# A second read of k in the last phase: its place in the DMA queue, and the rank of the gram's products on VectorE

## The chip, the cores and the metric

The kernel runs on one core of one Trainium2 chip. Its time is device microseconds of one execution, and the time that counts is the median of several. A core has TensorE (matrix products and transposes, into PSUM), VectorE and ScalarE (elementwise work, and copies out of PSUM), GpSimd (POOL; here little more than constants), and SyncE (SP), whose queue issues nearly all DMAs. An engine takes its instructions in the order in which the program has them, and so does a queue: an instruction that waits holds up what is behind it.

## The reference

The function is a residual block with two branches on a normalised input, and its gradients. S = 2048 rows, D = 512 channels, F = 1376 hidden channels, all in bf16:

```python
xn = layernorm(x)                                     # x = A_q
ks[s, d] = sum_j k[s - j, d] * shift_k[d, j]          # j = 0..3, a short causal filter
kv = ks * v
y = causal_convolution(kv, ssm_k) + kv * ssm_D        # over s, by FFT
A = xn * y
h = (xn @ w_gate) * (xn @ w_up)
B = h @ w_down
out = x + A + B
```

Ten tensors are returned: `out`, and for a given `grad_out` the gradients of x, k, v, shift_k, ssm_k, ssm_D and of the three weights. The part that matters here is the gradient of `shift_k`. With `dks` = d(loss)/d(ks), it is

`d_shift_k[d, j] = sum over s of dks[s, d] * k[s - j, d]`.

## The kernel before, in words

Sequence rows are spread over the 128 partitions, 16 consecutive rows (R) in each. The work has three stages: loading, normalising and the forward part of the convolution's transform; the hidden products of the second branch, block by block, with the spectral products between them; and a last phase, from about 316 us on, which computes the gradients of the weights.

In the last phase a generator `dw()` goes through 11 blocks (FBLK) of 128 hidden channels. For each it issues products for the gradient of `w_down` (`down_grad`, tile `pd`, L996), turns the hidden tensors of the next block by transposes (`hid_t`, tile `pt`, L840; from the loaded tile `hb`, two buffers, loaded at L787 two blocks ahead), and issues products for the gradients of `w_gate` and `w_up` (tile `pu`, L1032), which ScalarE copies to `og` (one buffer) and SP stores (L1043). `dw()` yields several times in a block, and at these points pieces of four other generators are put between, by a list `sides` of starting step and spacing:

- `inv_y` (from step 0, every third): the last step of the inverse transform, for four rows at a time. It takes the tiles `g1` (`load_g1`, L781, two buffers), first of y and then of the gradient `dd`, issues products `pq` (L913), and for the gradient VectorE forms `dks` = dd * v (L945) and `kb` = dd * ks (L946), which SP stores (L947). v and ks come by `load_vk` (L918, L920; two buffers). Eight g tiles are used so, two at a time; after them `load_dk` asks for the first two of four more.
- `dsk_gram` (from step 27, every second): the gradient of `shift_k`, for 128 channels at a time, two halves of 64 each. TensorE multiplies `dks` with four shifted views of k (tile `khC`, of 19 rows a partition: 16 of its own and 3 of the partition before) into a PSUM tile `pk` (L1055). The gradient is the diagonal of that product, so VectorE multiplies it by the identity, one product for each half (`kd`, L1060), and sums (L1062).
- `inv_dk` (from step 35): the gradient of the long filter `ssm_k`, from the four last g tiles (`po`, L971, into `o5t`). Its tile `o5t` has the memory of `khC` after it.
- `ew` (from step 10): `final(b)` (L1105 to L1122), the layer norm's backward pass and `out`, for two rows a piece, with a tile `bb` that it loads one piece ahead (L1094), and `bwd(b)` (L1084 to L1088), the gradient of k from `dks`. Both are VectorE's work, and SP stores what they make.

PSUM has a pool of three large buffers (`P2`), which `pu`, `pk`, `pt`, `pq` and `po` take in turn, and a pool of two smaller ones (`P1`, for `pd` and others). A tile's next user waits until the engine that reads it out has finished.

The order on each engine and queue is worked out at build time by a planner: it goes by the place in which an instruction is traced, as its priority, and by its own estimate of when things are ready. `tc.high_priority(offset=SOON)`, with SOON = 300, lets the instructions of a block count as if they had been traced 300 places earlier. `tc.issue_after(i)` adds the order that what the block issues on i's engine comes behind i; it does not say how soon.

`khC` is loaded by `load_kh` (L1126): a small memset on POOL and three requests on SP, 2048 KB for the rows themselves and 336 and 45 KB for the three rows from the partition before. `inv_y` calls it in its last pass, behind that pass's four requests of `load_vk`.

Of the kernel before, what the change touches and what calls it, by code (L numbers as in the profile page):

```python
# [11 lines left out]
ALU = mybir.AluOpType  # L12
ACTF = mybir.ActivationFunctionType
AX = mybir.AxisListType
# [6 lines left out]
R = 16  # L21
# [5 lines left out]
SOON = 300  # L27
# [163 lines left out]
def kernel(  # L191
# [24 lines left out]
    nc = tc.nc  # L216
# [20 lines left out]
    def dve(o, i):  # L237
        nc.vector.tensor_copy(o, i)  # L238
# [6 lines left out]
    GD = dram.tile([3, P, 2, R, D], BF, name="GD")  # L245
# [12 lines left out]
    ident = const.tile([P, P], BF, name="ident")  # L258
# [519 lines left out]

    def load_g1(sg, r0):
        t = CP["b"].tile([P, 2, 4, D], BF, name="g1")  # L780
        nc.sync.dma_start(t[:], GD[sg, :, :, r0:r0 + 4, :])  # L781
        return t

    def load_hb(fb):
        f0, fw = FBLK[fb]
        t = CP["b"].tile([P, NCH - 1, 3, 256], BF, name="hb")
        nc.sync.dma_start(t[:fw], HDD[:fw, fb])  # L787
        hbs[fb] = t
# [118 lines left out]
    dsk = c2.tile([P, NC4, 4], F32, name="dsk")  # L907
# [8 lines left out]
    def load_vk(r0):  # L916
        vb = c2b.tile([P, 2, D], BF, name="vb")
        nc.sync.dma_start(vb[:], v_n[:, r0:r0 + 2, :])  # L918
        kb = c2b.tile([P, 2, D], BF, name="kb")
        DKS["kb", r0] = nc.sync.dma_start(kb[:], KS[:, r0:r0 + 2, :])  # L920
        return vb, kb

    DKS = {}

    def inv_y():
        gq = pend
        todo = [(sg, r0) for r0 in range(0, R, 4) for sg in (0, 1)][2:]
        for r4 in range(0, R, 4):
            gy = gq.pop(0)
            vk = [load_vk(r4), load_vk(r4 + 2)]  # L930
            if r4 == R - 4:
                load_kh()
            for i in range(0, 4, 2):
                st1p(gy, i, yC[:, r4 + i:r4 + i + 2, :])
            if todo:
                gq.append(load_g1(*todo.pop(0)))
            yield
            gd = gq.pop(0)
            for i in range(0, 4, 2):
                r0 = r4 + i  # L940
                vb, kb = vk.pop(0)
                dd = c2b.tile([P, 2, D], BF, name="dd")
                st1p(gd, i, dd[:])
                with tc.high_priority(offset=SOON):
                    nc.vector.tensor_tensor(dks[:, r0:r0 + 2, :], dd[:], vb[:], op=ALU.mult)  # L945
                    nc.vector.tensor_tensor(kb[:], dd[:], kb[:], op=ALU.mult)  # L946
                DKS[r0] = nc.sync.dma_start(o3_n[:, r0:r0 + 2, :], kb[:])  # L947
                if r0 == 2:
                    nc.gpsimd.memset(dks[96:128, R:R + 3, :], 0.0)
                    nc.sync.dma_start(dks[0:112, R:R + 3, :], dks[1:113, 0:3, :])  # L950
                    nc.sync.dma_start(dks[112:127, R:R + 3, :], dks[113:128, 0:3, :])
            if todo:
                gq.append(load_g1(*todo.pop(0)))
            yield

    def load_gk(rq):
# [92 lines left out]
    def dsk_gram():  # L1049
        for c in range(NC4):  # L1050
            pk = P2("pk", [P, 2, D])
            for r in range(R):
                for h in range(2):
                    c0 = c * 128 + 64 * h
                    nc.tensor.matmul(pk[64 * h:64 * h + 64, h, 0:256], lhsT=dks[:, r, c0:c0 + 64],  # L1055
                                     rhs=KH[0][:, r:r + 4, c0:c0 + 64], start=(r == 0), stop=(r == R - 1))
            kd = c2.tile([P, 4, 64], F32, name="kd")
            for h in range(2):
                hs = slice(64 * h, 64 * h + 64)
                nc.vector.tensor_tensor(kd[hs], pk[hs, h, 0:256].rearrange("q (j c) -> q j c", j=4),  # L1060
                                        ident[hs, hs].unsqueeze(1).to_broadcast((64, 4, 64)), op=ALU.mult)
            nc.vector.tensor_reduce(dsk[:, c, :], kd[:], axis=AX.X, op=ALU.add)  # L1062
            yield
        dskb = c2.tile([P, 4, NC4], BF, name="dskb")
        nc.vector.tensor_copy(dskb[:], dsk[:].rearrange("q c i -> q i c"))
        for _ in range(2):
            yield
        pt = P1("pts", [P, 4, P], BF)
        for j in range(4):
            nc.tensor.transpose(pt[:NC4, j, :], dskb[:, 3 - j, :], ident[:])  # L1070
        dskt = c2.tile([NC4, P, 4], BF, name="dskt")
        dve(dskt[:], pt[:NC4].rearrange("c j q -> c q j"))
        nc.sync.dma_start(out_4.rearrange("(c p) j -> c p j", p=128), dskt[:])
        yield
# [51 lines left out]
    def load_kh():  # L1126
        khC = c2.tile([P, R + 3, D], BF, name="khC", tag="o5k")
        nc.gpsimd.memset(khC[0:1, 0:3, :], 0.0)
        with tc.issue_after(DKS["kb", R - 2].ins):
            nc.sync.dma_start(khC[:, 3:3 + R, :], k_n)  # L1130
            nc.sync.dma_start(khC[1:113, 0:3, :], k_n[0:112, R - 3:R, :])
            nc.sync.dma_start(khC[113:128, 0:3, :], k_n[112:127, R - 3:R, :])
        KH.append(khC)
# [63 lines left out]
```

## Time and profile before

| | |
|---|---|
| median of 3 runs | 487.18 us (486.45 to 489.52) |
| profiled execution | 485.22 us, span 483.4 us |
| TensorE busy (PE) | 471.3 us, 97% |
| VectorE busy (DVE) | 340.4 us, 70% |
| ScalarE busy (ACT) | 317.6 us, 66% |
| HBM traffic | 68.45 MB read, 63.41 MB written |
| granted TensorE clock | full throughout |

PE stands for TensorE's products, PEld for its weight loads, SPq for SP's queue. A row of the timeline has the start in us, the duration in us, the engine, the line, the operation, and the tiles as out<-in; in brackets, how long the engine stood idle ahead of it and what ended that. A row of waits has who waited, for what, the sum in us, how often, and the longest. The chain that ended last is the work followed back from the end, at each step to what released it. A row by stretches has the stretch, its length, the busy time of each engine with the number of instructions, the granted clock, the busy share of the DMA engines and the GB/s that they moved. For a DMA the time to landing counts from its issue.

### The profile page before, as it was taken

The page shows a single profiled execution, that of the slowest core. Times are in us where ns is not written, and L with a number is a line of the kernel's source. Part 1 is how long each engine was busy: PE and PEld are TensorE (multiplying, and loading weights), DVE is VectorE, ACT ScalarE, POOL GpSimd, SP SyncE. Part 2 cuts the span into 40 slices and gives each one's busy share as a digit, 9 for nine tenths or more (in the row PEclk, how much of TensorE's full clock was granted, in tenths as well). Part 3 has the DMA queues.
Part 4 walks back from the last instruction along what each step waited for, and adds up shares of the span by engine and source line. Part 5 has one row for each costly group of instructions (what it writes and reads, how often), then busy time and mean ns, then how long its engine had stood idle before and what let it go on. Part 6 is the DMA issues. An engine that isn't in the chain of part 4 may idle for free.

```text
span 483.4 us, 10516 instructions
## 1 busy us (share of the span) xinstructions
PE 471.3 (97%) x4335; PEld 314.5 (65%) x4335; DVE 340.4 (70%) x622; ACT 317.6 (66%) x354; POOL 15.3 (3%) x31
## 2 busy tenths in 40 slices
PE   7998998999999999999999999999999999999997
PEld 7866754647638547447447743566777787787885
DVE  7889969989275567686767866013257999999880
ACT  4976896759748778779779976275676535344241
POOL 8010000000000000000000000020000000000000
PEclk9999999999999999999999999999999999999999
DMA  9999998998997968967977378999999999599737
GB/s 269 378 381 354 294 263 298 353 311 315 327 288 260 263 201 269 280 203 248 287 238 262 119 270 317 381 329 313 318 383 380 320 374 414 199 250 241 229 147 247
DMA packets 105469, 139.87 MB, mean 289 GB/s; under 512 B 33323, under 2 KB 78800, under 8 KB 103758
## 3 DMA queue, kind: packets, MB, share of 16 engines
q1 hardware_dynamic: 103838, 137.84, 86.6%
q10 hardware_dynamic: 1584, 1.36, 1.0%
q8 instruction: 34, 0.56, 0.4%
q14 instruction: 13, 0.11, 0.1%
HBM read 68.45 MB, written 63.41 MB: 273 GB/s over the span
## 4 chain that ended last, share of the span: by engine, by line
PE 79%; DVE 9%; DMA 8%; ACT 1%; SPq 1%; issue 1%; DVEq 0%; ACTq 0%
PE pu L1032 15%; PE px L553 14%; PE pgu L510 13%; PE pd L996 7%; PE py L546 7%; PE pdh L516 6%; PE pt L840 4%; PE pq L913 3%; PE ps L582 3%; PE pg L611 3%; PE pf L368 2%; DMA HDD<-hd 2%; DVE fst L238 2%; PE pk L1055 2%; DMA out_dram<-og 1%; DMA kh<-in_A_k_dram 1%
## 5 line engine op out<-in xcount | busy, mean ns | idle before, releaser
L553 PE MATMUL px<-WT,hd 128*128 128x512 bf16 (+1 forms) x352 | 81.0, 380 | 0.0
L1032 PEld LDWEIGHTS <-xnC 128*128 128x128 bf16 x704 | 67.1, 98 | 8.8 <-issue 0.9
L553 PEld LDWEIGHTS <-hd 128*128 128x128 bf16 (+1 forms) x352 | 32.8, 98 | 44.2 <-issue 7.3
L1032 PE MATMUL pu<-natd,xnC 128*128 128x256 bf16 x512 | 58.5, 273 | 0.2 <-ACT nath L235 0.2
L235 ACT CAST GO<-pg 128x1024 bf16<-128x1024 f32 x48 | 46.2, 1015 | 13.4 <-issue 6.7
L598 DVE TENSOR_TENSOR T<-SP 128x2048 bf16<-128x2048 bf16 x24 | 29.3, 1222 | 34.8 <-ACT SP L235 34.8
L510 PE MATMUL pgu<-xt,Wu 128*128 128x256 bf16 (+1 forms) x352 | 53.2, 273 | 0.6 <-DVE fst L238 0.4
L235 ACT CAST gu<-pgu 128x1024 bf16<-128x1024 f32 (+1 forms) x48 | 45.4, 945 | 12.5 <-PE pgu L510 12.0
L235 ACT CAST SP<-ps 128x1024 bf16<-128x1024 f32 x48 | 46.5, 1027 | 10.3 <-PE ps L582 8.4
L510 PE MATMUL pgu<-xt,Wg 128*128 128x256 bf16 (+1 forms) x352 | 52.8, 273 | 0.0
L516 PE MATMUL pdh<-gt,WdT 128*128 128x256 bf16 (+1 forms) x352 | 47.1, 273 | 0.1
L510 PEld LDWEIGHTS <-Wu 128*128 128x128 bf16 (+1 forms) x352 | 33.0, 100 | 14.7 <-issue 10.2
L546 PE MATMUL py<-Wd,hd 128*128 128x512 bf16 (+1 forms) x176 | 41.4, 380 | 0.0
L235 ACT CAST og<-pu 128x1024 bf16<-128x1024 f32 (+1 forms) x11 | 10.9, 993 | 44.9 <-PE pu L1032 28.9
L235 ACT CAST fst<-pf 128x1024 bf16<-128x1024 f32 x40 | 39.0, 1032 | 0.8 <-ACT dh L235 0.5
L235 ACT COPY natd<-pt 128x2048 bf16<-128x2048 bf16 x16 | 30.0, 1874 | 13.1 <-PE pt L840 13.1
L516 PEld LDWEIGHTS <-WdT 128*128 128x128 bf16 (+1 forms) x352 | 34.9, 100 | 5.2 <-issue 0.2
L510 PEld LDWEIGHTS <-Wg 128*128 128x128 bf16 (+1 forms) x352 | 34.8, 100 | 3.9 <-DMA Wg<-in_B_w_gate_dram 0.3
L530 DVE TENSOR_TENSOR hd<-gu 128x512 bf16<-128x512 bf16 (+1 forms) x48 | 19.1, 397 | 19.5 <-ACT gu L235 19.5
L531 DVE TENSOR_TENSOR hd<-gu,dh 128x1024 bf16<-128x1024 bf16 (+1 forms) x48 | 30.8, 641 | 0.9
L996 PE MATMUL pd<-goC,nath 128*128 128x512 bf16 x128 | 30.1, 379 | 0.0
L546 PEld LDWEIGHTS <-hd 128*128 128x128 bf16 (+1 forms) x176 | 16.4, 98 | 20.5 <-issue 3.1
(171 smaller groups left out, 698.1 us busy)
## 6 DMA issues: line engine op xcount, KB each, us to landing
HDD<-hd SPq DMA_DIRECT2D x35, 384.0 KB, 4.2
FD<-fst SPq DMA_DIRECT2D x24, 512.0 KB, 4.8
X<-FD SPq DMA_DIRECT2D x24, 512.0 KB, 4.8
GD<-GO SPq DMA_DIRECT2D x24, 512.0 KB, 3.6
g<-GD SPq DMA_DIRECT2D x12, 1024.0 KB, 8.3
hb<-HDD SPq DMA_DIRECT2D x8, 1344.0 KB, 7.6
bb<-BX SPq DMA_DIRECT2D x8, 512.0 KB, 8.3
BX<-bx SPq DMA_DIRECT2D x7, 512.0 KB, 3.8
```

Source lines behind the costliest of these rows:

```text
L235: nc.scalar.copy(o, i)
L510: nc.tensor.matmul(pgu[:w, i, t, :], lhsT=W[:, c, f0:f0 + w], rhs=xt[:, :, c, :], start=(c == 0), stop=(c == NC4 - 1))
L516: nc.tensor.matmul(pdh[:w, i, :], lhsT=WdT[:, c, f0:f0 + w], rhs=gt[:, :, c, :], start=(c == 0), stop=(c == NC4 - 1))
L530: nc.vector.tensor_tensor(hd[:fw, fb0:fb0 + n, 0, :], gu[:fw, :n, 0, :], gu[:fw, :n, 1, :], op=ALU.mult)
L531: nc.vector.tensor_tensor(hd[:fw, fb0:fb0 + n, 1:3, :], gu[:fw, :n], dh[:fw, :n].unsqueeze(2).to_broadcast((fw, n, 2, 256)), op=ALU.mult)
L546: nc.tensor.matmul(py[:], lhsT=hd[:fw, fb, 0, ss], rhs=Wd[:fw, fb, :], start=(fb == 0), stop=(fb == NFB - 1))
L553: nc.tensor.matmul(px[:], lhsT=hd[:fw, fb, t, ss], rhs=W[:fw, fb, :], start=(t == 1 and fb == 0), stop=(t == 2 and fb == NFB - 1))
L582: nc.tensor.matmul(ps[32 * q:32 * q + 32, a, :], lhsT=TB.EF[64 * a:64 * a + 64, 4 * g + q, ri].rearrange("p k j -> p (k j)"), rhs=X[64 * a ...
L598: tt(W[:].rearrange("p c a d -> p c (a d)"), A[:, i:i + 1].rearrange("p c a d -> p c (a d)").to_broadcast((P, 2, 2 * D)), B[:].rearrange(" ...
L840: nc.tensor.transpose(pt[:, r, :fw], hs[:, (r % 2) * 128:(r % 2) * 128 + 128], ident[:fw, :fw])
L996: nc.tensor.matmul(pd[:fw, :], lhsT=nat_h(fb, r), rhs=goC[:, r, :], start=(r == 0), stop=(r == R - 1))
L1032: nc.tensor.matmul(pu[:, c, :, :fw], lhsT=xnC[:, r, cs(c)], rhs=nat_d(fb, r), start=(r == 0), stop=(r == R - 1))
```

## The change

There are two edits. `load_kh` is called one pass of `inv_y` earlier, at the end of the pass for rows 8 to 11, and its requests on SP are ordered behind the load of g that was traced last, in place of the last `kb` load of the last pass. At that point this load is the eighth and last g tile of `inv_y`, for the gradient of rows 12 to 15; the four of the long filter come later. The second edit puts the two products with the identity and the sum behind them, in each of the four pieces of `dsk_gram`, under `high_priority(offset=SOON)`. The arithmetic is the same.

```diff
     def load_g1(sg, r0):
         t = CP["b"].tile([P, 2, 4, D], BF, name="g1")
-        nc.sync.dma_start(t[:], GD[sg, :, :, r0:r0 + 4, :])
+        LG["g"] = nc.sync.dma_start(t[:], GD[sg, :, :, r0:r0 + 4, :])
         return t
+
+    LG = {}
...
         for r4 in range(0, R, 4):
             gy = gq.pop(0)
             vk = [load_vk(r4), load_vk(r4 + 2)]
-            if r4 == R - 4:
-                load_kh()
...
             if todo:
                 gq.append(load_g1(*todo.pop(0)))
+            if r4 == R - 8:
+                load_kh()
             yield
...
             kd = c2.tile([P, 4, 64], F32, name="kd")
-            for h in range(2):
-                hs = slice(64 * h, 64 * h + 64)
-                nc.vector.tensor_tensor(kd[hs], pk[hs, h, 0:256].rearrange("q (j c) -> q j c", j=4),
-                                        ident[hs, hs].unsqueeze(1).to_broadcast((64, 4, 64)), op=ALU.mult)
-            nc.vector.tensor_reduce(dsk[:, c, :], kd[:], axis=AX.X, op=ALU.add)
+            with tc.high_priority(offset=SOON):
+                for h in range(2):
+                    hs = slice(64 * h, 64 * h + 64)
+                    nc.vector.tensor_tensor(kd[hs], pk[hs, h, 0:256].rearrange("q (j c) -> q j c", j=4),
+                                            ident[hs, hs].unsqueeze(1).to_broadcast((64, 4, 64)), op=ALU.mult)
+                nc.vector.tensor_reduce(dsk[:, c, :], kd[:], axis=AX.X, op=ALU.add)
             yield
...
         nc.gpsimd.memset(khC[0:1, 0:3, :], 0.0)
-        with tc.issue_after(DKS["kb", R - 2].ins):
+        with tc.issue_after(LG["g"].ins):
             nc.sync.dma_start(khC[:, 3:3 + R, :], k_n)
```

## The prediction

> **What bounds the kernel now.** I read the page first: which engine is full, then the chain that ended last, then the last phase alone.
>
> ```profile
> span 483.4 us, 10516 instructions
> PE 471.3 (97%) x4335; PEld 314.5 (65%) x4335; DVE 340.4 (70%) x622; ACT 317.6 (66%) x354; POOL 15.3 (3%) x31
> ...
> PE 79%; DVE 9%; DMA 8%; ACT 1%; SPq 1%; issue 1%; DVEq 0%; ACTq 0%
> ```
>
> TensorE has work for 97% of the span and carries 79% of the chain. So a wait is worth something only where TensorE itself stands still. The list of waits for 386 to 484 us, where all products of the gram lie, has two waits of that kind:
>
> ```profile
> PE pt L840 <- DVE kd L1060: 0.7, 1, 0.7
> ...
> PE pu L1032 <- ACT nath L235: 0.2, 1, 0.2
> ```
>
> Shifted k is not in that list: no product waited for it. It is in time by little, though. The queue's timeline has the large request (L1130) at 379.44 us, and khC's rows show 10.4 us from issue to landing, so about 390.3 us; the first `pk` product starts at 391.35. The margin is 1.0 us in this execution.
>
> The 0.7 us is at 404.69, where a transpose needs the PSUM buffer of the second gram. VectorE's timeline shows why it is late (columns: start, duration, engine, line, instruction):
>
> ```profile
> 400.80 1.42 DVE L1119 SCALAR_TENSOR_TENSOR dxn<-xnC,m,dxn 128x512 f32<-128x512 bf16 x2
> 402.13 1.00 DVE L1120 TENSOR_SCALAR e<-dxn,rstd,m 128x512 bf16<-128x512 f32 x2
> 403.17 0.42 DVE L1060 TENSOR_TENSOR kd<-pk,ident 64x256 f32<-64x256 f32 x1
> 403.50 0.67 DVE L1121 TENSOR_TENSOR e<-e,goC 128x1024 bf16<-128x1024 bf16 x1
> 404.21 0.43 DVE L1060 TENSOR_TENSOR kd<-pk,ident 64x256 f32<-64x256 f32 x1
> ```
>
> The gram's products ended at 398.68; the two `kd` products ran behind work of `final(3)` and freed the buffer at 404.64. Everything that edit two can win in this execution is that 0.67 us.
>
> Third, the DMA rings, since edit one moves 2.49 MB (2048 + 336 + 45 KB). Of the table by stretches, in which the last two numbers are the DMA engines' busy share and the GB/s:
>
> ```profile
> 366.00:376.00 10.00, 10.00 (x98) 7.38 (x96) 8.13 (x19) 8.06 (x7) 0.00 (x0) 1.00 1.03 381
> ...
> 376.00:382.00 6.00, 6.00 (x48) 4.41 (x46) 5.86 (x10) 2.17 (x3) 0.00 (x0) 1.00 0.77 225
> ```
>
> Before 376 us the rings are full; behind it they have slack, and that is where shifted k is asked for today. The change takes it out of the slack and puts it into the full stretch.
>
> **The change part by part.** *Edit one: three requests of SP move up.* The g load after which they are now issued goes out at 364.86 (1.30 us), so they stand at about 366.2 to 367.6, ahead of these, and of the `vb` and `kb` at 377.5 to 379.0:
>
> ```profile
> 366.21 1.06 SPq L1094 DMA_DIRECT2D bb<-BX  x1
> 369.17 0.33 SPq L1107 DMA_DIRECT2D out_dram<-o  x1
> 369.60 0.60 SPq L787 DMA_DIRECT2D hb<-HDD  x1
> 375.64 0.33 SPq L1122 DMA_DIRECT2D out_dram<-e  x1
> ```
>
> The three issues cost SP 0.43 + 0.44 + 0.66 = 1.5 us; only `bb` moves by it, since `o` and `hb` waited longer than that for other things. The small POOL memset ran at 323.9, far ahead, and needs nothing new. What counts is the transfer: 2.49 MB at the 381 GB/s of that stretch is 6.5 us (5.9 at 424, the row of 374 to 376; 7.9 at 315, that of 370 to 372). Between 383 and 388, while shifted k's bytes move today, requests of 256 KB take 8.0 and 9.7 us to land; such requests at 409 to 412 take 4.9 and 3.6. So what is asked for behind it waits. [...]
>
> Step by step, with 6.5 us added:
> - the g load itself is ahead and lands as before, 364.86 + 8.3 = 373.2; its product starts at 376.33. No cost.
> - `bb` of `final(2)`: 366.21 + 8.3 = 374.5 becomes about 381. VectorE uses it at 377.33, so VectorE stops for some 3.5 us unless the planner has put other work there.
> - `hb` of block 5: 369.60 + 8.7 = 378.3 becomes 384.8. TensorE turns it at 385.90. In time by 1.1 us, where today it has 7.6. At 5.9 us the margin is 1.7; at 7.9 us TensorE waits 0.3.
> - the `vb` and `kb` of rows 12 to 15 land behind `hb`: stores and loads of 0.25 + 0.13 + 4 x 0.25 MB, some 3.7 us, so about 388.5 for the last. It landed at 378.97 + 5.0 = 384.0 and was used at 384.47. VectorE is then **4 us later** than today; `dks` is complete by 389, and the gram at 391.35 still finds it.
> - shifted k lands near 380, 11 us ahead of its use. In this execution that wins nothing; in one with slower DMAs, up to what exceeds the 1.0 us.
>
> SP runs in order and its stores wait for VectorE, so `hb` of block 6 moves from 391.46 to about 395.3. It is needed at 402.97, and the rings are emptier by then (shifted k is gone from 382 to 390), so 7.6 us to landing is just enough. No cost.
>
> *Edit two: precedence for eight products and four sums.* No work is added: 8 x 0.42 + 4 x 0.41 us of VectorE move. The trace can't show where the planner will place them; bounds: unmoved in order and 4 us late, minus the 0.5 us in which VectorE stood at 395.3, the second gram frees its buffer at 408.1 (+3.4 us of TensorE's waiting over today); right behind the gram with no lateness at 399.5 (-0.67). I take a place ahead of L1119, L1120 and L1121, that is 2.33 + 0.67 = 3.0 us earlier in the order, and 3.5 us of lateness: 404.64 - 3.0 + 3.5 = 405.1. TensorE could go on at 404.02, so it waits 1.1 us: **+0.4** against today. The first, third and fourth grams free buffers that nothing waits for; three to four microseconds later they still don't.
>
> *The end.* VectorE's lateness is eaten by its idle times behind 386 us: 0.50, 0.31, 0.43, 1.18 and 0.88, together 3.3 us, all ended by stores. The last two lie behind SP's transposes, which wait for TensorE, and are safe; the others may move along. So 0.6 to 1.9 us are left at the last `dk`. Its store stands right ahead of og's:
>
> ```profile
> 469.52 0.33 SPq L1088 DMA_DIRECT2D out_dram<-dk  x1
> 469.95 0.38 SPq L1004 DMA_DIRECT2D out_dram<-od  x1
> 470.43 0.91 SPq L978 DMA_DIRECT2D out_dram<-o5t  x2
> 471.42 2.17 SPq L1043 DMA_DIRECT2D out_dram<-og  x2
> ```
>
> ScalarE's last `og` copy at 477.04 waited for that store (one buffer), and the last og store, 478.3, ends only some half a microsecond ahead of the `od` store of 480.78 that ends the run. Later by 0.6 to 1.9, it ends the run 0.1 to 1.4 later.
>
> **Sum**: TensorE +0.4, the og path +0.1 to +1.4; they run side by side, so the larger counts: I take +0.4. The profiled execution took 485.22 us (span 483.4), 1.96 below the median of the runs, 487.18. So 485.6 by its count, and **487.6** beside the median.
>
> **Rivals.**
> 1. *VectorE is late and nothing takes it up* (slower). Place: the `kd` of the second gram and the og store. Price: up to 4 - 0.5 = 3.5 us at either, so 490.7. It decides when the added transfer exceeds about 6 us and the planner leaves `kd` where it is. For it: VectorE is busy 16.2 of 17 us from 386 to 403. Against it: the two idle times of 2.06 us behind the transposes. Within it, `hb` of block 5 is late too from 7.6 us of transfer on; by the 309 GB/s of the row of 388 to 390, 8.1 us, TensorE waits 0.5 us at 385.90.
> 2. *The stall goes and nothing is late*: loads pass shifted k, or the planner fills VectorE's wait with `bwd(0)`. Then -0.67 and, without lateness, perhaps the 0.2 behind it: 486.3. For it: `bwd(0)` has some 3 us of ready work right there.
> 3. *Runs without the profiler paid for shifted k's thin margin.* Their median is 2 us above the profiled execution. If a microsecond of it is TensorE waiting at 391.35, the change wins it on top of 2: 485.5. Against it: nothing in this trace shows it.
> 4. *Nothing moves*: the planner issues k no earlier, `kd` stays: 487.2.
>
> **Chances.** Forecast (within 0.8 us of 487.6) 0.45; rival one 0.22; two 0.18; three 0.08; four 0.07. The range 485.8 to 490.0 leaves out the far end of rival one and most of three. One per cent, 4.9 us, is about what a measurement of this kernel can tell from no change: only rival one with its prices added (4 us at VectorE plus the wait for `hb`) comes there; slower by more 0.04, faster by more 0.01, within 0.95.
>
> **What would show it.** Right: shifted k asked for near 366 and landed by 381; VectorE waiting for `bb` near 377 and for `vb` or `kb` near 385; no TensorE wait at the first `pk`; a wait for `kd` near 404 of about a microsecond; the last `dk` store a microsecond later. Wrong: VectorE on time at 386, or the `kd` wait gone (rival two), or a TensorE wait on `hb` near 386 (rival one).

## The result, and the profile after

The changed kernel takes 489.38 us (median of 22 runs, 487.12 to 493.43); the kernel before, run beside it, 487.26 us (22 runs, 485.11 to 493.17). The ratio is 1.0043, with an interval of 1.0024 to 1.0063: about 2.1 us slower, clear of noise, and well inside one per cent. The profiled execution took 489.37 us, so it stands for the median; that of before (485.22) lies 2.0 us under its own. Between the two profiles there are 4.15 us, twice what the medians differ by: the profile before is of a fast execution, that after of a middling one, and this has to be kept in mind wherever the two are laid side by side.

The page of the changed kernel, its busy line and the chain that ended last by engine:

```profile
span 487.5 us, 10518 instructions
PE 473.8 (97%) x4335; PEld 315.8 (65%) x4335; DVE 340.5 (70%) x622; ACT 318.0 (65%) x354; POOL 15.4 (3%) x31
...
PE 72%; DMA 15%; DVE 9%; ACT 1%; SPq 1%; issue 1%; DVEq 0%; ACTq 0%
```

No engine got more work, since the counts are the same. TensorE is busy 2.5 us longer with the same products, and DMAs carry 15% of the chain in place of 8%. Where TensorE waits, the waits between 366 and 488 us tell (lines of L1030 and up have moved by 3, those around L840 and L971 by 2):

```profile
PE po L973 <- DMA g<-GD: 2.0, 1, 2.0
...
PE pt L842 <- DMA hb<-HDD: 0.5, 1, 0.5
...
PEld L842 <- DVE kd L1063: 0.4, 1, 0.4
```

The wait for `kd` is gone as a wait of the products. Two waits for DMAs are there in its place: 0.5 us for `hb` of block 5, and 2.0 us for the last tile of g.

**Where shifted k went.** SP's queue in the changed kernel, around the place of the edit:

```profile
365.76 0.64 SPq L781 DMA_DIRECT2D g<-GD  x1
366.45 1.74 SPq L1133 DMA_DIRECT2D khC<-in_A_k_dram  x1
...
369.63 0.38 SPq L1097 DMA_DIRECT2D bb<-BX  x1
...
377.43 0.34 SPq L1125 DMA_DIRECT2D out_dram<-e  x1
377.86 0.38 SPq L789 DMA_DIRECT2D hb<-HDD  x1
```

The three requests stand where the prediction put them, 366.45 to 369.6. The large one landed 13.7 us after its issue, at 380.1, the second at 381.4. Of the kernel before only the second's landing is known, 390.3, 10.4 us after its issue at 379.92. What the prediction did not have is the last two lines: the planner now puts the store of `e` ahead of `hb`. That store waits for VectorE, so `hb` is asked for at 377.86 in place of 369.60, and with 9.1 us to landing it comes at 387.0. By stretches (columns: stretch, length, busy time and count of each engine, granted clock, DMA share, GB/s):

```profile
366.00:376.00 10.00, 10.00 (x96) 7.18 (x94) 6.38 (x16) 8.20 (x7) 0.00 (x0) 1.00 1.04 399
376.00:382.00 6.00, 6.00 (x50) 4.60 (x48) 5.43 (x9) 2.22 (x3) 0.00 (x0) 1.00 0.99 313
```

The slack of 376 to 382 (0.77 busy, 225 GB/s before) is used up. VectorE forms the last `dks` at 391.46, in place of 383.87. The work around it is less late: 3.7 us at the end of `final(3)` (403.50 before, 407.16 after), and still 2.4 us at the last `dk`.

Not all of that is the change's doing. VectorE's first row that stands in another place than before is at 376 us. Ahead of it, at the same product of `final(2)`, it was already 1.8 us late, the first line from the kernel before, the second from the changed kernel:

```profile
367.73 0.69 DVE L1105 TENSOR_TENSOR o<-xnC,yC 128x1024 bf16<-128x1024 bf16 x1 [3.32 <-DMA out_dram<-o]
```

```profile
369.52 0.69 DVE L1108 TENSOR_TENSOR o<-xnC,yC 128x1024 bf16<-128x1024 bf16 x1 [4.21 <-DMA out_dram<-o]
```

It waits for an earlier store of `o`, which SP issued at 361.66 in place of 360.17, before it came to shifted k. So 1.5 of the 1.8 us can't come from the early request; whether the rest does isn't known. Seven profiles here are of kernels whose VectorE and SP still have the order of the kernel before at this point, that one included: they have this product between 367.73 and 370.45, and the profile before has the earliest. From there to the end of `final(3)` the changed kernel loses another 1.9 us: 1.0 because a second wait for a store of `o` is longer (1.54 us at 383.18, 0.50 at 395.77 before), and some 0.8 because `kd` work now stands ahead of it.

**Where the end comes from.** SP's queue from 433 to 459 us, in the kernel before:

```profile
433.77 0.29 SPq L1073 DMA_DIRECT2D out_dram<-dskt  x1
...
434.55 12.88 SPq L801 DMA_TRANSPOSE natT<-HDD  x2
447.52 0.54 SPq L1004 DMA_DIRECT2D out_dram<-od  x1
...
455.00 1.00 SPq L1043 DMA_DIRECT2D out_dram<-og  x2
456.09 0.56 SPq L781 DMA_DIRECT2D g<-GD  x1
```

and after:

```profile
436.87 0.29 SPq L1076 DMA_DIRECT2D out_dram<-dskt  x1
...
438.38 11.67 SPq L803 DMA_TRANSPOSE natT<-HDD  x2
450.15 0.54 SPq L1006 DMA_DIRECT2D out_dram<-od  x1
...
456.97 0.33 SPq L1091 DMA_DIRECT2D out_dram<-dk  x1
457.40 1.00 SPq L1045 DMA_DIRECT2D out_dram<-og  x2
458.49 0.55 SPq L781 DMA_DIRECT2D g<-GD  x1
```

Read it from the top. The stores of `dskt`, `e` and `o` wait for VectorE and are late. The two transposing loads behind them go in 3.8 us later and come out 2.6 us later: only 1.2 us of the lateness is taken up there. Behind them SP issues a store of `dk` (448.16 before, 450.78 after), and VectorE needs the buffer that this store frees. The first line is from before, the second from the changed kernel:

```profile
450.48 0.69 DVE L1084 TENSOR_TENSOR dk<-dks,skb 128x1024 bf16<-128x1024 bf16 x1 [1.18 <-DMA out_dram<-dk]
```

```profile
454.45 0.69 DVE L1087 TENSOR_TENSOR dk<-dks,skb 128x1024 bf16<-128x1024 bf16 x1 [1.91 <-DMA out_dram<-dk]
```

The next `dk` that VectorE finishes is stored at 456.97, and og's stores and the last load of g stand behind that, 2.4 us later than before. Before, that tile landed at 461.81, and its product started at 461.96 without a wait, with 0.15 us to spare:

```profile
461.96 1.06 PE L971 MATMUL po<-IW,g 128*128 128x128 bf16 x16
```

In the changed kernel TensorE has done what lies ahead, and stands:

```profile
461.85 0.59 PE L998 MATMUL pd<-goC,nat 128*128 128x512 bf16 x2
464.44 0.23 PE L973 MATMUL po<-IW,g 128*128 128x128 bf16 x1 [2.00 <-DMA g<-GD]
```

The wait isn't all of it. The stretches behind it, in the same columns as above:

```profile
464.00:465.00 1.00, 0.56 (x7) 0.57 (x8) 0.97 (x2) 0.05 (x1) 0.00 (x0) 0.81 0.83 310
465.00:466.00 1.00, 1.00 (x13) 1.00 (x11) 0.97 (x2) 0.00 (x0) 0.00 (x0) 0.50 0.00 0
...
467.00:468.00 1.00, 1.00 (x7) 0.67 (x5) 0.97 (x2) 0.25 (x1) 0.00 (x0) 0.50 0.00 0
468.00:469.00 1.00, 1.00 (x11) 0.89 (x10) 0.97 (x2) 0.00 (x0) 0.00 (x0) 0.99 0.56 211
```

From about 464.6 to 468.0, some 3.4 us, TensorE is granted half its clock. Measured against the same products in the profile before, it loses another 1.6 us there. So TensorE's lateness against the profile before runs like this: +0.4 us already before the place of the change (the two executions differed there), +0.7 at `hb`, -0.8 where the `kd` wait was, +2.2 at g, +1.6 in the half clock: +4.1, which is the span's 487.5 - 483.4.

### The profile page after: what moved, and what is told of

Its sections match the earlier page's. It is cut to its first block, busy times and chain, and to the rows that moved or that the text cites. A ratio compares the mean times of both kernels' runs of the same rounds, so it can differ in the third digit from the quotient of the medians.

```text
span 487.5 us, 10518 instructions
## 1 busy us (share of the span) xinstructions
PE 473.8 (97%) x4335; PEld 315.8 (65%) x4335; DVE 340.5 (70%) x622; ACT 318.0 (65%) x354; POOL 15.4 (3%) x31
## 4 chain that ended last, share of the span: by engine, by line
PE 72%; DMA 15%; DVE 9%; ACT 1%; SPq 1%; issue 1%; DVEq 0%; ACTq 0%
PE pu L1034 13%; PE px L553 13%; PE pgu L510 13%; PE py L546 6%; PE pdh L516 6%; DMA hb<-HDD 6%; PE pd L998 5%; PE pt L842 3%; PE ps L582 3%; PE pg L611 3%; PE pf L368 2%; DMA HDD<-hd 2%; DVE fst L238 2%; DMA out_dram<-o 2%; PE pk L1057 2%; PE pq L915 1%
```

## The experiments

**Theory A.** Both edits make VectorE late, and that lateness is handed on by SP's queue, which runs in order (`hb` went out 8.3 us later once it stood behind the store of `e`): stores, transposing loads, stores, the last load of g. TensorE pays at g, and pays again in clock. **Rivals:** the bytes of k alone cost, at `hb` of block 5, and g is only a symptom; the cost is in og's stores at the end; each edit has a price of its own and the two add. Each kernel was run beside the kernel before on the same chip; the rows come from four such groups of runs, so rows with another "before there" are compared by their ratios. The ratio isn't the quotient of the two medians beside it (for edit two alone that would be 1.0061). The last column counts the runs in which the mean granted clock fell below 0.999. It is a weak sign of a TensorE wait: the mean goes over the whole span, and half clock behind TensorE's last product, while the last stores land, lowers it too (to 0.998 and 0.997 in two profiles).

| kernel | median us | before there | ratio, 95% | clock below 0.999 |
|---|---|---|---|---|
| both edits (the changed kernel) | 489.38 | 487.26 | 1.0043 [1.0024, 1.0063] | 11 of 22 |
| edit one alone | 488.51 | 486.33 | 1.0029 [0.9998, 1.0059] | 8 of 12 |
| edit two alone | 489.31 | 486.33 | 1.0043 [1.0017, 1.0069] | 8 of 12 |
| both, last two g on ScalarE's queue | 489.64 | 486.33 | 1.0057 [1.0030, 1.0084] | 8 of 12 |
| before, last two g on ScalarE's queue | 490.67 | 486.33 | 1.0068 [1.0039, 1.0096] | 11 of 12 |
| before, six more products on VectorE | 492.37 | 487.24 | 1.0102 [1.0065, 1.0138] | 6 of 6 |
| both, VectorE relieved of 11 us | 486.69 | 487.24 | 0.9994 [0.9961, 1.0027] | 6 of 12 |
| before, VectorE relieved of 11 us | 486.88 | 487.24 | 0.9995 [0.9964, 1.0026] | 5 of 12 |
| both, 24 stores on POOL's queue | 516.22 | 487.24 | 1.0590 [1.0551, 1.0630] | 6 of 6 |
| both, last `po` later | 489.15 | 487.43 | 1.0030 [1.0002, 1.0057] | 11 of 12 |
| edit two, last `po` later | 487.74 | 487.43 | 0.9990 [0.9960, 1.0019] | 8 of 12 |
| before, last `po` later | 486.23 | 487.43 | 0.9973 [0.9941, 1.0005] | 3 of 12 |
| both, one of 16 rows of k loaded | 488.01 | 487.43 | 1.0008 [0.9977, 1.0039] | 5 of 12 |

The kernel before itself fell below 0.999 in 10 of 35, 6 of 23 and 15 of 35 of its runs on the three chips of the experiments, and those runs were 1.0 to 1.9 us longer in the median than its others.

### Edit one alone

The products with the identity are left as they were.

```diff
-            with tc.high_priority(offset=SOON):
-                for h in range(2):
...
+            for h in range(2):
```

> Edit one alone: shifted k asked for early, the gram's products on VectorE without precedence. Theory A (the early transfer makes VectorE late by some 3 us, SP's stores wait for VectorE, and the last load of g behind them reaches TensorE late): slower than the kernel before by 1.5 to 4 us, a TensorE wait for g of 1 to 3 us near 462 us, and besides a wait for kd near 405 of 1 us or more, since nothing moves kd forward. Rival B (what costs is the hidden tile hb of block 5, which now stands behind shifted k in the ring): slower by no more than its own wait near 387, 0.5 to 1.1 us. Rival C (the precedence reorders VectorE, and that makes the stores late): no slower than before.

The median is 2.2 us above that of before (1.4 us by the ratio), with an interval that reaches just under no change. Its profile has both DMA waits, as the list between 366 and 490 us shows:

```profile
PE po L973 <- DMA g<-GD: 2.1, 1, 2.1
...
PE pt L842 <- DMA hb<-HDD: 1.5, 1, 1.5
```

There is no wait for `kd` in it, although `kd` keeps its old rank: with `hb` 1.5 us late, TensorE comes to that transpose later itself.

### Edit two alone

```diff
-            for h in range(2):
...
+            with tc.high_priority(offset=SOON):
+                for h in range(2):
...
```

> Edit two alone: precedence for the gram's products, shifted k where it was. Theory A and rival B: faster than the kernel before by 0 to 0.7 us, the wait for kd near 404.7 gone, no TensorE wait for g beyond 0.3 us. Rival C: slower by 1 us or more, with a TensorE wait for g near 462.

Theory A expected a gain here, and so did rival B; the time is the one that rival C named, slower by 1 us or more (2.1 us by the ratio) with a wait for g. The stall for `kd` is gone; TensorE gains 0.8 us where it was. SP's queue and then TensorE's timeline of this kernel:

```profile
457.63 0.56 SPq L781 DMA_DIRECT2D g<-GD  x1
```

```profile
463.57 1.07 PE L971 MATMUL po<-IW,g 128*128 128x128 bf16 x16 [2.21 <-DMA g<-GD]
```

g is asked for 1.5 us later than before, and TensorE comes to it 0.6 us earlier. The 1.5 us don't come from the edit. VectorE was as late at 369.20 already, on a store of `o`:

```profile
369.20 0.69 DVE L1106 TENSOR_TENSOR o<-xnC,yC 128x1024 bf16<-128x1024 bf16 x1 [4.32 <-DMA out_dram<-o]
```

In this kernel SP's requests have the order of the kernel before to the end, and VectorE's instructions have it up to 401 us. From that product to the request for g there are 88.43 us here and 88.36 before. `kd` ahead of `final(3)` delays VectorE by some 0.6 us at the end of `e`, but nothing of that is left at g. So rival C's mechanism, stores made late by the new order, isn't in this profile, and neither is theory A's. What edit two changes at g is that TensorE is there earlier and finds less of a margin; the lateness of the load is this execution's own.

The runs without the profiler show that edit two alone does cost. Edit one costs 1.4 us by its ratio and edit two 2.1, both together 2.1, so the third rival, prices that add, isn't what these figures say; but their intervals are wide enough to leave room for it.

### The last two g loads on ScalarE's queue, with both edits and before

This takes g out from behind SP's stores; nothing else is asked for differently.

```diff
-    def load_g1(sg, r0):
+    def load_g1(sg, r0, q=None):
...
-        LG["g"] = nc.sync.dma_start(t[:], GD[sg, :, :, r0:r0 + 4, :])
+        LG["g"] = (q or nc.sync).dma_start(t[:], GD[sg, :, :, r0:r0 + 4, :])
...
-                    gks.append(load_gk(rq + 2))
+                    gks.append(load_gk(rq + 2, nc.scalar))
```

> Both edits, and the two last loads of g for the long filter asked for on ScalarE's queue, right behind the copy that frees the tile, so that they stand behind no store of VectorE's. Theory A: the TensorE wait for g near 462 is gone and with it the half clock behind it; 2 to 4 us faster than the changed kernel where that shows the wait in full, so within 1 us of the kernel before; the last stores still 1 to 2 us late. Rival B: at most 0.3 us from the changed kernel, the wait for hb near 387 stays and the time with it. If VectorE's lateness costs by the og stores alone, the time stays 1 to 2 us above the kernel before.

> The kernel before, with the two last loads of g on ScalarE's queue. Theory A: the load lands 1 to 4 us ahead of its product in place of 0.1 us, so an execution in which it came late gains; 0 to 1.5 us faster than the kernel before. Rival B: no difference beyond 0.3 us.

The wait for g goes in both, and no time is won in either: 489.64 and 490.67. With both edits TensorE waits 25 us earlier instead, where a transpose needs what VectorE makes of the gram's sums:

```profile
439.48 0.22 PE L989 MATMUL ptd<-ident,dDs 128*4 128x128 bf16 x1 [2.46 <-DVE dskt L238]
```

and half clock (0.50) follows, from 440.9 to 444.3. That wait is for the most part the experiment's own: g is asked for at 425.0 in place of 433.3, a store of `o` issued right behind that frees its buffer later, and VectorE stands 2.71 us for it at 431.84, where the changed kernel's profile has no idle time; the gram's sums (`dskt`) come 2.6 us later than there. In the kernel before, the loss is on SP. The planner, with g gone from the queue, put a store of `o` ahead of the transposing loads:

```profile
438.89 0.36 SPq L1107 DMA_DIRECT2D out_dram<-o  x1
439.34 10.25 SPq L801 DMA_TRANSPOSE natT<-HDD  x2
...
457.62 0.33 SPq L1088 DMA_DIRECT2D out_dram<-dk  x1
458.05 1.00 SPq L1043 DMA_DIRECT2D out_dram<-og  x2
```

They go in 4.8 us later than before, og's stores 3.1 us later, and the last copy of `og` waits 8.96 us for its buffer. TensorE's last product ends 0.3 us later than in the profile before, the run 2.9 us later: here the stores of `og` set the end. That the wait for g goes is as theory A has it; that no time follows is not. The experiment changed the order of SP as well as g's queue, so it doesn't tell what g's wait alone costs.

### The last g product later: the wait without its queue

Here only TensorE's order is changed. The first products of the last g tile go one step later, into the middle of a `pu` group. The queues keep their order.

```diff
-                sd[0] += sd[1]
+                sd[0] += sd[1] + (sd is sides[2] and n == 53)
```

> Both edits, and on TensorE alone the first products with the last g tile come one place later, between the two halves of a pu group, 3.6 us of work further on; the order on every other engine and queue is that of the changed kernel. Theory A, as it stands now (VectorE's lateness reaches TensorE through the last load of g, and a wait of some 2 us there also costs a stretch at half the granted clock): no wait for g near 462, granted clock of 0.999 or more in most executions, 1.5 to 3 us faster than the changed kernel. Rival D (VectorE's lateness reaches the end through the og stores in any case): less than 0.7 us faster, the last og store as late as in the changed kernel.

> Edit two alone with the same later place of those products; VectorE, ScalarE and SP in the order of edit two alone. Theory A: 1.5 to 3 us faster than edit two alone, within 0.7 us of the kernel before or faster, the wait for kd still gone. If VectorE is again 1.5 us late from 367 us on in the profile, that lateness belongs to the order and not to one execution's DMAs. Rival D: within 0.7 us of edit two alone.

> The kernel before with the same later place of those products, as the partner of the two runs above. Theory A: 0 to 1 us faster than the kernel before, with fewer executions at a granted clock below 0.999. Rival D: no difference.

For edit two the ratio falls from 1.0043 to 0.9990, some 2.6 us, though g is asked for later still (459.79). That is what one expects if its price was the wait for g: in this execution it would have been 2.4 us, since TensorE passed the old place at 463.12, the tile landed at 465.49 and was used at 466.62. But the kernel before gains by the later place too, 0.9973, and against this partner on the same chip edit two is still 0.8 us slower by the ratios and 1.5 by the medians, which isn't clear of noise. So the price at g is the likeliest reading and not proved, and up to some 2 us may come from elsewhere.

The profile names one such place. VectorE was 2.7 us later at `o` (370.45) than in the profile before, again ahead of any change of order: the expectation had taken a second late start as a sign of the order, but the rows of SP and VectorE up to there are in the order of the kernel before, so it belongs to the execution. Late as it is, the last copy of `og` waits 6.1 us for its buffer, till 482.11. TensorE's last product ends 1.2 us later than in the profile before (481.1), the span 3.6 us later (487.0); og's stores set the end, as rival D had it. The low clock of this execution lies there as well, behind all work of TensorE:

```profile
485.00:486.00 1.00, 0.00 (x0) 0.00 (x0) 0.00 (x0) 0.00 (x0) 0.00 (x0) 0.50 0.44 91
```

The largest wait of TensorE is now one that the change's first edit aims at:

```profile
393.28 1.94 PE L1055 MATMUL pk<-khC,dks 128*64 128x256 bf16 x32 [1.71 <-DMA khC<-in_A_k_dram]
```

With both edits the wait for g is gone too (the tile landed at 466.24 and was used at 469.25), but the time is 489.15, hardly less. In its profile TensorE waits for `hb`, longer than in the changed kernel's, with half clock from 388.7 to 392.1:

```profile
389.14 1.67 PE L842 MATMUL pt<-ident,hb 128*128 128x128 bf16 x14 [2.58 <-DMA hb<-HDD]
```

The two waits stand in for each other. In this execution TensorE came by at the old place of the `po` products (a `pu` product starts there) at 465.76, 0.5 us ahead of the landing: late by `hb`, it would hardly have waited for g. So with edit one the wait for `hb` is a price of its own. The runs agree: on this chip, with the later place in both, edit one on top of edit two costs 1.4 us by the medians and 2.0 by the ratios, just clear of noise. The kernel before with the later place takes 486.23, the fastest whole kernel here, 1.2 us under before; its interval reaches 1.0005, so it isn't proved to be faster.

### Is it the bytes of k?

The changed kernel with one of the 16 rows of k in each partition loaded (128 KB in place of 2.49 MB) and the rest of `khC` set to zero. The gradient of `shift_k` is therefore left incomplete.

```diff
-        nc.gpsimd.memset(khC[0:1, 0:3, :], 0.0)
+        nc.gpsimd.memset(khC[:], 0.0)
...
-            nc.sync.dma_start(khC[:, 3:3 + R, :], k_n)
-            nc.sync.dma_start(khC[1:113, 0:3, :], k_n[0:112, R - 3:R, :])
-            nc.sync.dma_start(khC[113:128, 0:3, :], k_n[112:127, R - 3:R, :])
+            nc.sync.dma_start(khC[:, 3:4, :], k_n[:, 0:1, :])
```

> Both edits, but of k only one row of 16 a partition is loaded (128 KB in place of 2429), the rest of the tile is zeroed on GpSimd far ahead: the early request stays, its bytes go, and the gradient of shift_k is computed from the wrong k. Theory A: hb of block 5 and the vb and kb loads land as early as in the kernel before, no wait for hb near 387, VectorE on time at 385, the time that of edit two alone or up to 1 us less. If the bytes are not what makes VectorE late: bb, vb and kb land as late as in the changed kernel.

The median is 488.01, a ratio of 1.0008. SP's queue has the old order again:

```profile
369.74 0.38 SPq L789 DMA_DIRECT2D hb<-HDD  x1
375.78 0.34 SPq L1125 DMA_DIRECT2D out_dram<-e  x1
```

VectorE forms the last `dks` at 384.01 (before: 383.87), g is asked for at 454.83 (456.09), and neither `hb` nor g has a wait. The only waits are for `kd`, 0.78 and 1.40 us: the planner has put the second gram's `kd` behind `final(3)`'s last product here, precedence or not, so the run doesn't carry edit two as the changed kernel does, and its time can't be set against that of edit two alone. What it does show is that the bytes, and not the early place of a request on SP, make `hb` and `dks` late. The other profiles bear it out: counted from the product of `final(2)` above, the last `dks` comes 16.1 to 16.8 us later in the eight profiles without the bytes ahead, and 21.9 to 22.8 in the five with them (that with the stores on POOL left out). One point is only argued: `hb`'s place behind the store of `e` is the planner's, which reckons with the size of the transfer; that the order changes back with the bytes is seen, why is not.

### Is it VectorE's lateness?

First, the lateness alone, without either edit: six more products of 0.69 us on VectorE, traced ahead of the last rows of `dks`, in the kernel before. Their result is not used. The planner spread them: one came ahead of each of the last two products for `dks`, the others behind these.

```diff
+                    if r0 == R - 4:
+                        late = c2.tile([P, 2, D], BF, name="late")
+                        for _ in range(6):
+                            nc.vector.tensor_tensor(late[:], dd[:], vb[:], op=ALU.mult)
                     nc.vector.tensor_tensor(dks[:, r0:r0 + 2, :], dd[:], vb[:], op=ALU.mult)
```

> The kernel before, with six more products of 128x1024 on VectorE (into a tile that nobody reads) right ahead of dks of row 12: 6 x 0.69 = 4.1 us of lateness from 383 us on, no DMA and no order of the k load touched. Theory A (VectorE, through SP's in-order queue, has no slack towards the end): 1.5 to 4 us slower than the kernel before, the store of dskt and with it the transposing loads on SP later by more than 1 us, and TensorE waiting for g near 462 or the last og stores later by 2 us or more. Rival B (VectorE has slack, TensorE alone sets the end): within 0.5 us of the kernel before.

The six products, which follow one another every 0.60 us, put VectorE 3.6 us back and cost 5.1 us at the end, 1.0102. The waits of TensorE are elsewhere than in the changed kernel:

```profile
393.73 1.94 PE L1059 MATMUL pk<-khC,dks 128*64 128x256 bf16 x32 [1.85 <-DVE dxn L1123]
410.36 1.68 PE L840 MATMUL pt<-ident,hb 128*128 128x128 bf16 x14 [3.89 <-DVE kd L1064]
```

The second line is rival one of the prediction at its place: a late VectorE and a `kd` that nothing moves forward. TensorE stood for 3.89 us, and half clock came with it, 0.50 from 409.8 to 413.3. The first wait has little to do with VectorE: the products read `khC` and `dks`, not the tile named; `dks` had been formed by 387.8, and the second request of shifted k had landed at 393.43. So it is most likely k's thin margin again. g had no wait here, since TensorE itself came later. Of the 3.6 us VectorE's idle times took up 1.0 by the last `dk`.

Then the opposite. In the changed kernel and in that before, the gradient of k is formed of three taps in place of four, 16 products and sums of 0.69 us fewer on VectorE.

```diff
-        for j in range(4):
+        for j in range(3):
             src = dks[:, 2 * b + j:2 * b + j + 2, :]
```

> Both edits, and one of the four taps left out of the gradient of k in bwd: 16 operations of VectorE, some 11 us, of which about 6 lie ahead of 450 us. Theory A: with VectorE relieved the two edits cost nothing any more: no TensorE wait for g, within 0.7 us of the same reduction of the kernel before, and 1.5 to 4 us faster than the changed kernel. Rival B (what is left is the transfer ahead of hb of block 5): still 0.5 to 1 us slower than the reduced kernel before, with a TensorE wait near 387. Rival C (precedence costs by the planner's order): still 1.5 us or more slower than the reduced kernel before.

> The kernel before with the same tap left out, as the partner of the run above. Theory A: 0 to 2 us faster than the kernel before, since its VectorE is late in part of the executions; the last dk store some 8 us earlier. If VectorE has slack: no difference.

Now the two kernels take the same, 486.69 with the edits and 486.88 without. Neither waits for g or for `kd`. What is left is one wait in each, the first line from the kernel with the edits, the second from that without:

```profile
389.61 0.95 PE L842 MATMUL pt<-ident,hb 128*128 128x128 bf16 x14 [2.00 <-DMA hb<-HDD]
```

```profile
392.82 1.94 PE L1055 MATMUL pk<-khC,dks 128*64 128x256 bf16 x32 [1.17 <-DMA khC<-in_A_k_dram]
```

Edit one exchanges a wait for k against a wait for `hb`. The margins of these ratios against the kernel before are about 1.6 us either way, so a cost of a microsecond would not be seen in them; the cost of the full change, 2.1 us, shows no trace. This bears on the tail, not on `dks`: with the edits the last `dks` is as late as ever in the profile (394.1), and what the relief takes away is VectorE's lateness at the end.

### The late stores on another queue

If SP hands the lateness on, the stores of `o`, `e` and `dk` could go where nothing waits behind them.

```diff
-        nc.sync.dma_start(o2_n[:, rb, :], dk[:])
+        nc.gpsimd.dma_start(o2_n[:, rb, :], dk[:])
...
-        nc.sync.dma_start(o0_n[:, rb, :], o[:])
+        nc.gpsimd.dma_start(o0_n[:, rb, :], o[:])
...
-        nc.sync.dma_start(o1_n[:, rb, :], e[:])
+        nc.gpsimd.dma_start(o1_n[:, rb, :], e[:])
```

> Both edits, with the stores of final and bwd (o, e, dk: 24 of them) on GpSimd's queue, which has nothing else to do there, so that SP waits for VectorE no more. Theory A: the transposing loads and the g loads go out 2 us or more earlier than in the changed kernel, no TensorE wait for g near 462, 2 to 4.5 us faster than the changed kernel, about 0.7 us faster than the kernel before if the kd wait is gone too. Against it stands what GpSimd takes to issue a store, which no run has shown: if it slows VectorE, no gain. Rival B: no gain beyond 0.5 us.

516.22 us, 29 us slower. The 24 stores take POOL from 15.4 to 28.5 us busy, 0.55 us each, and they now wait in one line for one another's results:

```profile
POOL out_dram L1125 <- DVE e L1124: 65.5, 8, 11.3
...
POOL out_dram L1091 <- DVE dk L1090: 44.7, 8, 9.8
...
DVE e L1112 <- DMA out_dram<-e: 14.9, 4, 5.6
```

VectorE waits for its buffers behind stores that stand behind other stores, and TensorE then for `kd` (7.9 us), `dks` (6.2) and g (4.6). The order of the stores on POOL's queue is the planner's. Whether it or the queue itself costs this much was not separated, so the experiment says nothing on theory A beyond that a late VectorE is dear.

### What the experiments leave

Shown for edit one: the bytes delay `hb` and `dks`, in every profile that has them early. TensorE waits for `hb` in four of these five (0.5 to 2.6 us) and in none of the others, and with g out of the way edit one, on top of edit two, costs 1.4 to 2.0 us in the runs. For edit two it is shown that the runs are slower, and that the time comes back where g's products stand later; that the price lies at g is the likeliest reading, with its partner's gain and the noise against it. Theory A as it stands, lateness of VectorE made by the edits and handed on, isn't shown to be the cause: of the 2.4 us by which g is asked for late in the changed kernel's profile, 1.8 stood at 369.5, within what executions of the same order differ by, and 0.6 came later (1.2 in two other profiles with edit one). The profiles before and after thus overstate it. The rival that made `hb` everything fails by edit two, which has no such wait. That og's stores are the cost fails for the changed kernel's profile: og's last stores went out at 481.48, and the `od` store behind TensorE's last product, 484.91, ends the run. It doesn't fail in general, since two profiles without the wait for g end by og's stores. How the 2.1 us of the unprofiled runs divide between `hb`, g and og's stores isn't settled. A kernel that asks for k behind `hb`, where it should delay neither, wasn't tried.

## Why the prediction was right or wrong

The time, 489.4, is 1.8 us above the 487.6 that was forecast and 1.3 below the 490.7 of rival one; it lies in the range, and within one per cent as expected. That it does is in part luck: the waits in the profile after, for `hb` by an order that wasn't foreseen and for g with half clock behind it, are in neither of the two sums. Most of what the prediction said of single transfers held, and one step failed.

- *k and its bytes.* Right. Asked for at 366.45 to 369.6, landed at 380.1 against "near 380", the second request at 381.4. The loads behind it were late: the first `vb` and `kb` took 7.8 and 7.2 us to land, 3.7 and 4.1 before. That each of them comes later by the transfer's whole 6.5 us was an estimate, and no run shows it by itself. (The 10.4 us to landing were read off the second request's row and not the large one's; the landing at 390.3 and the margin of 1.0 us are right for the second.)
- *`bb`.* The 3.5 us were put under the proviso of other work, and the planner had it: VectorE's timeline shows `bwd(0)` from 377.32 to 381.6, then 1.54 us of idle time, for the store of `o` and not for `bb`.
- *`hb` of block 5.* Predicted to land at 384.8 with 1.1 us to spare. It landed at 387.0, since the planner put the store of `e` ahead of it. Its issue was taken as unmoved. By the sum's bytes alone it would have been in time; the order was not foreseen. The wait is 0.5 us in this profile, 1.5 to 2.6 in three others, and none in one.
- *VectorE 4 us later.* The size came out, 3.7 us at the end of `final(3)`, by luck: VectorE never waited for `vb` or `kb`, since the planner put the rest of `final(2)` ahead of `dks`. The 3.7 us are 1.8 that stood at 369.5, 1.0 for a store of `o`, and 0.8 of `kd` work moved ahead. The last `dks` came at 391.46, not by 389, but the first `pk` product ran at 392.39 without a wait of its own.
- *`kd`.* Predicted free of its wait to 1.1 us left. VectorE's timeline of the changed kernel has it at its new rank, ahead of L1122 to L1124:

```profile
403.44 0.86 DVE L1063 TENSOR_TENSOR kd<-pk,ident 64x256 f32<-64x256 f32 x2
...
407.16 0.69 DVE L1124 TENSOR_TENSOR e<-e,goC 128x1024 bf16<-128x1024 bf16 x1
```

  The buffer came free at 404.30 instead of 405.1, and TensorE, itself 1.1 us late by then, needed it no earlier. The term was +0.4; TensorE's lateness against before fell by 0.8 there instead.
- *The end: the step that failed.* The sum let VectorE's idle times eat its lateness: "The last two lie behind SP's transposes, which wait for TensorE, and are safe." In the changed kernel SP came to the transposes 3.8 us late by VectorE's own stores, with TensorE only 0.3 us late there, and out of them 2.6 us late. So what ends the first of the two idle times came 4.0 us later (454.45 in place of 450.48), and that idle time grew from 1.18 to 1.91 us and took nothing up. That, and a load that was not in the sum: the last tile of g stands on SP behind stores of VectorE's results and two of og, some 15 us ahead of the ones that the prediction followed, and had 0.15 us of margin (461.81 to 461.96). The list of waits before held the hint, a weight load that waited 0.2 us for g, and it was not read as a margin. At the stores that the prediction did follow the lateness was above the 0.6 to 1.9 us forecast, 2.4 us at the last `dk` and 3.6 at the last og stores, but TensorE was later still.
- *Granted clock.* No term of the sum had it. It nearly doubled the price: 2.0 us of waiting cost 3.6 in this profile.
- *Rival one.* "VectorE is late and nothing takes it up" was right on the lateness; it named the `kd` of the second gram and the og store as the place. The run with a delayed VectorE shows the first place at work where `kd` has its old rank, and the profile of edit two with the later `po` the second. In the changed kernel's profile the place is g.
- *Rival three.* k's thin margin is real: of the seven profiles with shifted k asked for late, five show TensorE waiting 0.64 to 1.85 us at the first `pk` products, three of them (1.17, 1.40 and 1.71 us) with shifted k named as what ended the wait. But the edit did not win it, because `hb` pays instead.
- *The base.* The profile before was 2.0 us under its median, and adding the difference to the median was right: the changed kernel's profile shows 4.15 us more, the medians 2.1. What the prediction couldn't see from one profile is that its margins belong to an execution in which VectorE was early.

## What to carry to other kernels

Before moving a large transfer ahead on a queue that runs in order, list every load that stands behind the delayed engine's stores, down to the end of the kernel, with its landing and first use side by side; a weight load's wait of 0.2 us is a margin of nothing (the margin at g was 0.15 us). When two profiles are laid side by side, find the first row whose order differs, and take off what one of them is late by ahead of it: that is not the change. Don't count an idle time as a buffer because something else ends it: ask how late the work ahead may be before that no longer ends it. Where TensorE is 97% busy, as here, a wait of 2 us can cost nearly twice its length (the 2.0 us at g cost 3.6, while another wait of 2.00 us left the clock full); take waits of such a kernel as exchanged rather than removed until the profile after shows otherwise.

## What the runs showed of the hardware

In these profiles the granted clock falls to one half around the end of a wait of about 2 us or more, between 0.5 us ahead of that end and 1.4 us behind it, and stays there for about 3.4 us. In thirteen profiles (all but that with the stores on POOL), TensorE's waits from 380 us on that were 0.5 to 1.85 us long left the clock full (ten of them); of two waits of 2.00 us one did and one did not; the five of 2.06, 2.21, 2.46, 2.58 and 3.89 us all brought it to 0.50, for 3.4 us each time that it was counted from the rows.

The mean clock of a run doesn't tell where the half clock lay. In the profiles of the kernel before with g on ScalarE's queue (0.998) and of edit two with the later `po` (0.997) the clock is full as long as TensorE works; it falls to 0.50 some 4.5 and 3.2 us behind its last product, while the last stores land. In ten of the eleven changed or altered kernels that have runs of both kinds, the runs with a mean clock below 0.999 are 1.6 to 4.5 us longer in the median than the others of that kernel (in two of them there is only one run to compare with); in the eleventh, edit two with the later `po`, they are no longer than the others. A long tail makes a run longer as a wait does, so these counts don't say which it was. The kernel before, whose profile shows a full clock throughout its work, falls there in a quarter to two fifths of its runs.

Transposing loads hold what is behind them on their queue: a pair of them on SP took 12.9 us in the kernel before and 11.7 in the changed one, and the next request went out 0.1 us behind their end in both, while a plain request in the rows shown took 0.3 to 1.7.
